# Loading v for four strips at once, in 128 partitions, in a fused attention and two-layer MLP kernel

## Chip, cores, metric

The kernel runs on one core of one Trainium2 chip. The metric is the time of one execution on the device, in microseconds (us), as the median of several executions of the same program. Less is better.

## What is computed

Sliding-window attention over 4 batches, 8 heads, 576 positions and 64 dimensions; then two MLP layers on the 2304 x 512 result. Half of the heads see the last 32 positions, the other half every fourth of the last 128 (the host reorders these heads' positions, so that they too see 32 neighbours of their own residue class).

```python
scores = np.matmul(q, k.transpose(0, 1, 3, 2)) / np.sqrt(64)
mask_plain = (rel >= 0) & (rel < 32)
mask_dil = (rel >= 0) & (rel < 128) & (rel % 4 == 0)
attn = softmax(np.where(mask, scores, -1e9))
x = np.matmul(attn, v)                      # to (2304, 512)
h = x @ w_in;  x = (h * sigmoid(1.702 * h)) @ w_out      # 512 -> 2048 -> 512
h = x @ w_in2; x = (np.maximum(h, 0) ** 2) @ w_out2      # 512 -> 2048 -> 512
```

## The kernel before

**Attention.** A batch is done in four groups (`SUBS0` for the first batch, `SUBS` for the others). A group is four strips of 32 queries that move along together: two head pairs k and the two halves u of the sequence, over `nw` = 4 or 5 windows of 32 positions. `pp` = 0 or 1 says which two head pairs (plain or dilated). Strip number a takes the partitions 32a to 32a+31 of every tile of the group; before, a = 2u + k. Groups 0 to 3 are those of the first batch, groups 4 to 7 those of the second. `attend` emits for each group:

- scores (L573): per window 8 small fp32 matmuls, of which each shows as two in the trace;
- a masked running minimum on DVE (L591), an exponential on ACT (L598), per window and head of the pair;
- reciprocals on DVE (L636, L639), a scaling on POOL for the first batch (L646, two per group), a 32x32 transpose on DVE (L660);
- values (L683): `nw`+1 steps of 8 small matmuls; step i reads the 32 keys of window i of all four strips, `v_of(a, i)`;
- evacuation of the result into the MLP's input x, in pieces: the high part by ACT or DVE (L313, L315), the low part by DVE (L700).

**v.** The keys of the first batch lie in two tiles (`v_first`, one for each pp, called `first` in the trace, as the q and k of that batch are). `load_v0` brings one strip with one load: 32 partitions, 4 packets of 1536 bytes each, eight loads for the batch (L862). Groups of later batches use one buffer `v`, filled by four loads of 32 partitions and 3 packets of 1024 bytes (`load_v`, L538); their q and k come with four loads (L530). All these loads are issued by SP, in one queue with the loads of the first layer's weights.

**MLP, layer 1.** A weight block of 128 x 512 comes as two 32-bit words per number, one load of 512 KB into one of three `raw` buffers (L379). ACT or DVE makes the top half (`c`, L313), DVE joins it (L390), ACT or DVE rounds the high part into `wp` (L313), DVE takes the low part (L324), and only then is the `raw` buffer free. There are 32 such blocks, (f, part) with f = 0 to 15; part 0 feeds L737 to L739 (hidden), part 1 feeds L794 to L796 (projection). The first layer goes through five blocks of tokens, the first with 512 tokens; the weights come in during the first. Layer 2 prepares its weights during layer 1 and runs from some 288 us on.

**Order.** Nothing is ordered by hand: a list scheduler (`Schedule`) runs over all tasks when the program is built, with costs and due times per task (`OFF`, `LEAD`, `V_FROM`, ...), and emits each engine's instructions in the order in which its plan starts them. Each engine and each queue then runs strictly in that order on the chip, with semaphore waits. Where the plan leaves PE idle before the first MLP matmul, it emits matmuls on zeros (L909, "warm" matmuls): idle time divided by `IDLE[1]`.

Of the kernel before, what the change touches and what calls it, by code (L numbers as in the profile page):

```python
# [40 lines left out]
T_ATT = 1.76  # L41
A0 = 0.23
A1 = 1.02
# [16 lines left out]
RAW_FROM = 2.32  # L60
NEXT_FROM = 20.56
OFF = (0.0, -2.48, 0.0, 0.0, 0.0, 0.0, 0.0, 0.0, 0.0, 0.0, 14.46, 0.0, -3.56, -7.14, -5.19, 0.23, -13.95, 0.0, 6.66, -22.66, 0.0, -0.52, -0.81, -0.26)
SHIFTED = ()
WARM = 256
QK_FROM = -40
QK_STEP = 4.03
V_FROM = -22.0
V_STEP = 10.52
LEAD = (22.67, 7.05, 3.53)
SPACE = 4.99  # L70
C_BUFS = 2
RAW_BUFS = 3
IDLE = (0.25, 0.22)
SPARE_POOL = (0.51, 0, 3.41)
SPARE_ACT = (0.24, 0.36, 0)
SPARE_TO = (51.64, 211.81)

# [28 lines left out]
PATIENCE = {"pe": 0.02, "act": 0.02, "dve": 0.02, "pool": 0.02, "dma": 0.02, "host": 0.02}  # L106
X_EARLY = 17.0
X_FROM = 3.56
# [147 lines left out]
def attention_mlp_mlp(  # L256
# [37 lines left out]
    q_other = [staged(f, 2 * (UQ + UK)).rearrange("p (k c) -> p k c", k=2) for f in (7, 5)]  # L294
    v_first = [staged(f, 4 * NBLK * P).rearrange("k (t d) -> k t d", t=4 * NBLK) for f in (6, 5)]
    sm_first = [staged(6, 10 * KW) for _ in range(4)]
# [210 lines left out]
    def attend(b, pp, spec, nw, want, n0, loads=None):  # L507
# [10 lines left out]
        if first:  # L518
            d_qk, d_v = loads["qk"], loads["v"]
            qk_bs = v_bs = []  # L520
        else:
            qk_bs, v_bs = [buffer("qk")], [buffer("v")]

            def load_qk(h):
                if "qk" not in m:
                    m["qk"] = qkv.tile([P, 4, 2, 6 * WIN], F32, tag="qk", bufs=1, name="qk")
                (u, w0), n = spec[h], WIN * (nw + 1)
                src = qkv_in[b, p0:p0 + 2, u, :, WIN * w0:WIN * w0 + 2 * UQ].rearrange("k p (t c) -> p k t c", t=2)
                for t in range(2):
                    nc.sync.dma_start(m["qk"][:, 2 * h:2 * h + 2, t, 0:n], src[:, :, t, 0:n])  # L530

            def load_v(h, k):
                if "v" not in m:
                    m["v"] = qkv.tile([P, 6, P], F32, tag="v", bufs=1, name="v")
                (u, w0), a, at = spec[h], WIN * (2 * h + k), UQ + UK
                c, i = (0, 0) if w0 == 0 else (1, 1)
                src = qkv_in[b, p0 + k, u, WIN * c:WIN * (c + 3), at + P * i:at + P * (i + 2)].rearrange("(c k) d -> k c d", k=WIN)
                nc.sync.dma_start(m["v"][a:a + WIN].rearrange("k (c i) d -> k c (i d)", c=3), src)  # L538

            d_qk = [  # L540
                task("dma", moved_in(512, 128 * (nw + 1)), want - 6, lambda h=h: load_qk(h), (), qk_bs, since=NEXT_FROM, count=2)
                for h in range(2)
            ]
            d_v = [
                task("dma", moved_in(96, 1024), want - 2, lambda h=h, k=k: load_v(h, k), (), v_bs, since=NEXT_FROM)
                for h in range(2) for k in range(2)
            ]

        def rows_of(a, i, wide):
            u, w0 = spec[a // 2]  # L550
            if not first:
                return m["qk"][:, a, wide, WIN * i:WIN * (i + 1 + wide)]
            w = WIN * (w0 + i)
            if pp == 0:
                return q_plain[a // 2][:, a % 2, wide, w:w + WIN * (1 + wide)]
            at = w + UQ * wide
            return q_other[u][:, a % 2, at:at + WIN * (1 + wide)]

        def v_of(a, i):
            if first:  # L560
                t = spec[0][1] + i
                v, at = v_first[pp], 4 * NBLK - 1 if t == 3 * NBLK else t % 3 * NBLK + t // 3
            else:
                v, at = m["v"], i % 3 * 2 + i // 3
# [107 lines left out]
        def values():  # L672
# [4 lines left out]
            for i in range(nw + 1):  # L677
                lo, hi = max(0, i - 1), min(nw, i + 1)
                for a in range(4):
                    rows = slice(a * WIN, (a + 1) * WIN)  # L680
                    for j in range(2):
                        js = slice(D * j, D * (j + 1))
                        T.matmul(  # L683
                            m["o"][a // 2][js, a % 2, lo * WIN:hi * WIN], v_of(a, i)[:, js],
                            pt[rows, j, max(0, i * KW - WIN):min(nw * KW, i * KW + WIN)],
# [149 lines left out]
    def spread_masks(part):  # L835
# [3 lines left out]
        if part == 0:  # L839
            G.tensor_copy(mask_band[:, 2], mask_band[:, 1])  # L840
            G.tensor_copy(mask_band[P // 2:P, 1], mask_band[P // 2:P, 0])

# [15 lines left out]

    def load_v0(pp, u, k, on):
        a, at = WIN * (2 * u + k), UQ + UK  # L860
        src = qkv_in[0, 2 * pp + k, u, :, at:].rearrange("(c q) d -> q c d", q=WIN)
        on.dma_start(v_first[pp][a:a + WIN].rearrange("q (c i) d -> q c (i d)", c=4), src)  # L862

# [3 lines left out]
    def by_act(want, fn, count=1):  # L867
# [12 lines left out]
        for u in range(2)  # L880
    ]
    v0 = [
        [
            early(moved_in(128, 1536), V_FROM + V_STEP * pp + OFF[(8, 10)[u] + pp], lambda u=u, k=k, pp=pp: load_v0(pp, u, k, nc.sync))
            for u in range(2) for k in range(2)
        ] for pp in range(2)
    ]
    loads0 = [
        {"qk": halves[0], "v": v0[0]}, {"qk": halves[0] + halves[1], "v": v0[0]},
        {"qk": others[0] + others[1], "v": v0[1]}, {"qk": others[0] + others[1], "v": v0[1]},  # L890
    ]
# [644 lines left out]
```

## Time and profile before

| | us |
|---|---|
| median of 3 runs | 813.61 (813.29 to 814.11) |
| the profiled execution | 811.69 |
| its span, first to last instruction | 809.9 |
| PE busy in the span | 796.2 |
| DVE, ACT busy | 532.2, 407.2 |
| first MLP matmul (L737) starts | 31.44 |

The span is what the views below are measured in; 1.8 us of the profiled execution lie around it. PE is busy nearly throughout. The warm matmuls count as busy too, so the share of the first 31 us says nothing of useful work. Where a view names a wait, it names what ended it.

### The profile page before, as it was taken

The page shows a single profiled execution, that of the slowest core. Times are in us where ns is not written, and L with a number is a line of the kernel's source. Part 1 is how long each engine was busy: PE and PEld are TensorE (multiplying, and loading weights), DVE is VectorE, ACT ScalarE, POOL GpSimd, SP SyncE. Part 2 cuts the span into 40 slices and gives each one's busy share as a digit, 9 for nine tenths or more (in the row PEclk, how much of TensorE's full clock was granted, in tenths as well). Part 3 has the DMA queues.
Part 4 walks back from the last instruction along what each step waited for, and adds up shares of the span by engine and source line. Part 5 has one row for each costly group of instructions (what it writes and reads, how often), then busy time and mean ns, then how long its engine had stood idle before and what let it go on. Part 6 is the DMA issues. An engine that isn't in the chain of part 4 may idle for free.

```text
span 809.9 us, 16451 instructions
## 1 busy us (share of the span) xinstructions
PE 796.2 (98%) x6559; PEld 721.8 (89%) x6559; DVE 532.2 (66%) x1162; ACT 407.2 (50%) x931; POOL 9.3 (1%) x22
## 2 busy tenths in 40 slices
PE   6899999999999999999999999999999999999998
PEld 4688887888899988888888999999999999999998
DVE  3788875443355588788887655689455698365774
ACT  6678775444444554544444255445355445354432
POOL 3000000000000000000000000000000000000000
PEclk9799999999999999999999999999999999999999
DMA  9666764221232379888576933695867687677751
GB/s 257 184 225 211 234 188 146 60 54 40 53 112 75 102 229 304 308 290 334 189 275 240 347 118 121 253 367 208 333 245 291 255 318 244 239 271 280 276 191 59
DMA packets 67964, 172.64 MB, mean 213 GB/s; under 512 B 5680, under 2 KB 43568, under 8 KB 62512
## 3 DMA queue, kind: packets, MB, share of 16 engines
q1 hardware_dynamic: 67168, 171.25, 61.4%
q8 instruction: 51, 0.84, 0.4%
q10 hardware_dynamic: 720, 0.34, 0.1%
q14 instruction: 25, 0.20, 0.1%
HBM read 132.78 MB, written 38.80 MB: 212 GB/s over the span
## 4 chain that ended last, share of the span: by engine, by line
PE 87%; DMA 8%; DVE 2%; ACT 2%; issue 1%; ACTq 0%; SPq 0%
PE ps L1225 7%; PE ps L1378 7%; PE ps L1380 7%; PE ps L1223 7%; PE ps L1224 7%; PE ps L1379 7%; PE ps L737 7%; PE ps L738 7%; PE ps L739 7%; PE ps L794 7%; PE ps L795 7%; PE ps L796 7%; DMA raw<-in_w 5%; DMA first<-in_qkv 2%; PE ps L683 2%; PE ps L573 1%
## 5 line engine op out<-in xcount | busy, mean ns | idle before, releaser
L737 PE MATMUL ps<-x,wp 128*128 128x512 f32 (+1 forms) x320 | 119.4, 373 | 0.4 <-DVE x L700 0.4
L794 PE MATMUL ps<-gh,wp 128*128 128x512 f32 (+1 forms) x320 | 119.1, 372 | 0.0
L738 PE MATMUL ps<-x,wp 128*128 128x512 f32 (+1 forms) x320 | 117.9, 368 | 0.0
L795 PE MATMUL ps<-gh,wp 128*128 128x512 f32 (+1 forms) x320 | 117.8, 368 | 0.0
L739 PE MATMUL ps<-x,wp 128*128 128x512 f32 (+1 forms) x320 | 117.8, 368 | 0.0
L796 PE MATMUL ps<-gl,wp 128*128 128x512 f32 (+1 forms) x320 | 117.7, 368 | 0.0
L1380 PE MATMUL ps<-gl,ws 128*128 128x384 f32 x336 | 112.2, 334 | 0.0
L1378 PE MATMUL ps<-gh,ws 128*128 128x384 f32 x336 | 112.2, 334 | 0.0
L1379 PE MATMUL ps<-gh,ws 128*128 128x384 f32 x336 | 112.2, 334 | 0.0
L313 ACT CAST gh<-gq 128x768 fp32r<-128x768 f32 x84 | 68.8, 837 | 70.4 <-PE ps L1379 49.5
L324 DVE TENSOR_TENSOR gl<-gq,gh 128x768 fp32r<-128x768 f32 x84 | 80.4, 957 | 28.3 <-PE ps L1380 22.1
L1223 PE MATMUL ps<-xo,ws 128*128 128x384 f32 x252 | 84.2, 334 | 0.0
L1224 PE MATMUL ps<-xo,ws 128*128 128x384 f32 x252 | 84.2, 334 | 0.0
L1225 PE MATMUL ps<-xo,ws 128*128 128x384 f32 x252 | 84.2, 334 | 0.0
L769 DVE SCALAR_TENSOR_TENSOR g<-g,ps 128x512 f32<-128x512 f32 (+1 forms) x80 | 50.4, 629 | 48.4 <-ACT g L766 47.9
L766 ACT ACTIVATE g<-ps 128x512 f32<-128x512 f32 (+1 forms) x80 | 44.0, 551 | 73.3 <-PE ps L739 72.6
L737 PEld LDWEIGHTS ps<-x,wp 128*128 128x128 f32 x320 | 60.3, 188 | 11.9 <-DVE x L700 0.9
L794 PEld LDWEIGHTS ps<-gh,wp 128*128 128x128 f32 x320 | 60.2, 188 | 10.3
L739 PEld LDWEIGHTS ps<-x,wp 128*128 128x128 f32 x320 | 60.3, 188 | 10.0
L796 PEld LDWEIGHTS ps<-gl,wp 128*128 128x128 f32 x320 | 60.3, 188 | 10.1
L795 PEld LDWEIGHTS ps<-gh,wp 128*128 128x128 f32 x320 | 60.3, 188 | 9.8
L738 PEld LDWEIGHTS ps<-x,wp 128*128 128x128 f32 x320 | 60.3, 189 | 9.7
(83 smaller groups left out, 1338.6 us busy)
## 6 DMA issues: line engine op xcount, KB each, us to landing
ws<-wo_s SPq DMA_DIRECT2D x42, 1024.0 KB, 7.0
raw<-in_w SPq DMA_DIRECT2D x64, 511.8 KB, 4.5
ws<-wi_s SPq DMA_DIRECT2D x36, 896.0 KB, 6.5
wo_s<-wt SPq DMA_DIRECT2D x16, 896.0 KB, 6.3
wi_s<-wt SPq DMA_DIRECT2D x16, 896.0 KB, 5.5
v<-in_qkv SPq DMA_DIRECT2D x48, 96.0 KB, 2.9
qk<-in_qkv SPq DMA_DIRECT2D x24, 192.0 KB, 3.8
xs<-x2d SPq DMA_DIRECT2D x12, 384.0 KB, 4.8
```

Of the source, the lines that this page charges most:

```text
L737: T.matmul(out, w_hi[:, ks], x[:, 0, k, a:z], start=(k == 0), stop=False)
L738: T.matmul(out, w_hi[:, ks], x[:, 1, k, a:z], start=False, stop=False)
L739: T.matmul(out, w_lo[:, ks], x[:, 0, k, a:z], start=False, stop=(k == KD - 1))
L794: T.matmul(out, w_hi[:, ds_], m["gh"], start=(f == 0 and a == 0), stop=False)
L795: T.matmul(out, w_lo[:, ds_], m["gh"], start=False, stop=False)
L796: T.matmul(out, w_hi[:, ds_], m["gl"], start=False, stop=(f == KF - 1))
L1223: T.matmul(out, wt[:, 0, a, ks], hi, start=(first and k == 0), stop=False, skip_group_check=True)
L1224: T.matmul(out, wt[:, 0, a, ks], lo, start=False, stop=False, skip_group_check=True)
L1225: T.matmul(out, wt[:, 1, a, ks], hi, start=False, stop=(k == 1), skip_group_check=True)
L1378: T.matmul(out, w[:, 0, j, ds_], hi, start=(first and j == 0), stop=False, skip_group_check=True)
L1379: T.matmul(out, w[:, 1, j, ds_], hi, start=False, stop=False, skip_group_check=True)
L1380: T.matmul(out, w[:, 0, j, ds_], lo, start=False, stop=(j == NPR - 1), skip_group_check=True)
```

## The change

Strip a now belongs to head pair k = a // 2 and half u = a % 2. With that, the four strips of a group lie in the input at equal distances, (k, u) by (k, u), and one load can bring the same 32 keys of all four strips: 128 partitions with one packet each. The first batch has, for each pp, three loads of 128 packets of 1536 bytes (`c` = 0 to 2) and one of 128 packets of 512 bytes (`c` = 3, the tenth window, which only groups 1 and 3 read); before, the tile held two windows twice. Later groups have three loads of 128 packets of 1024 bytes instead of four of 96. The source of such a load has the pattern 4 blocks (126,976 elements apart) x 32 rows (992 apart) x 384 elements, its destination 128 partitions x 384; before, both sides had 32 x 4 x 384.

```diff
-A0 = 0.23
+A0 = 0.22
...
-LEAD = (22.67, 7.05, 3.53)
+LEAD = (20.53, 4.91, 2.03)
...
-IDLE = (0.25, 0.22)
+IDLE = (0.25, 0.18)
...
-    v_first = [staged(f, 4 * NBLK * P).rearrange("k (t d) -> k t d", t=4 * NBLK) for f in (6, 5)]
+    v_first = [staged(f, (NWIN + 1) * P).rearrange("k (t d) -> k t d", t=NWIN + 1) for f in (6, 5)]
...
-            def load_v(h, k):
+            def load_v(c):
...
-                (u, w0), a, at = spec[h], WIN * (2 * h + k), UQ + UK
-                c, i = (0, 0) if w0 == 0 else (1, 1)
-                src = qkv_in[b, p0 + k, u, WIN * c:WIN * (c + 3), at + P * i:at + P * (i + 2)].rearrange("(c k) d -> k c d", k=WIN)
-                nc.sync.dma_start(m["v"][a:a + WIN].rearrange("k (c i) d -> k c (i d)", c=3), src)
+                at, i = UQ + UK, int(spec[0][1] > 0)
+                row = WIN * (c + i)
+                src = qkv_in[b, p0:p0 + 2, :, row:row + WIN, at + P * i:at + P * (i + 2)].rearrange("k u q d -> (k u) q d")
+                nc.sync.dma_start(m["v"][:, 2 * c:2 * c + 2].rearrange("k i d -> k (i d)"), src)
...
-                            m["o"][a // 2][js, a % 2, lo * WIN:hi * WIN], v_of(a, i)[:, js],
+                            m["o"][a % 2][js, a // 2, lo * WIN:hi * WIN], v_of(a, i)[:, js],
...
-            G.tensor_copy(mask_band[P // 2:P, 1], mask_band[P // 2:P, 0])
+            for a in (1, 3):
+                G.tensor_copy(mask_band[WIN * a:WIN * (a + 1), 1], mask_band[WIN * a:WIN * (a + 1), 0])
...
-    def load_v0(pp, u, k, on):
-        a, at = WIN * (2 * u + k), UQ + UK
-        src = qkv_in[0, 2 * pp + k, u, :, at:].rearrange("(c q) d -> q c d", q=WIN)
-        on.dma_start(v_first[pp][a:a + WIN].rearrange("q (c i) d -> q c (i d)", c=4), src)
+    def load_v0(pp, c):
+        at, i = UQ + UK, c // 3 * (NBLK - 1)
+        src = qkv_in[0, 2 * pp:2 * pp + 2, :, WIN * c:WIN * (c + 1), at + P * i:at + P * NBLK].rearrange("k u q d -> (k u) q d")
+        nc.sync.dma_start(v_first[pp][:, NBLK * c:NBLK * (c + 1) - i].rearrange("k i d -> k (i d)"), src)
...
-        {"qk": halves[0], "v": v0[0]}, {"qk": halves[0] + halves[1], "v": v0[0]},
-        {"qk": others[0] + others[1], "v": v0[1]}, {"qk": others[0] + others[1], "v": v0[1]},
+        {"qk": halves[0], "v": v0[0][0:3]}, {"qk": halves[0] + halves[1], "v": v0[0]},
+        {"qk": others[0] + others[1], "v": v0[1][0:3]}, {"qk": others[0] + others[1], "v": v0[1]},
```

`rows_of` and `v_of` follow the new numbering. Seven planner constants and eight of the 24 entries of `OFF` have new values, and the scheduler's plan comes out anew: all engines' orders change. The number of instructions does not, but for 12 v loads fewer on SP in the later groups, one POOL copy more, and 82 warm matmuls where 63 stood.

**SP's queue at the start of the program**, before (`first` at L862 are the v loads of the first batch, `raw` the weight blocks, `qk` and `v` those of group 4):

```order
L877 DMA first<-in_qkv 128x2x608 x2
L862 DMA first<-in_qkv 32x4x384 x8
L379 DMA raw<-in_w 128x2047 x3
L530 DMA qk<-in_qkv 128x2x160 x4
L538 DMA v<-in_qkv 32x3x256 x2
L379 DMA raw<-in_w 128x2047
```

and now:

```order
L878 DMA first<-in_qkv 128x2x608 x2
L863 DMA first<-in_qkv 128x1x384 x6
L379 DMA raw<-in_w 128x2047
L863 DMA first<-in_qkv 128x1x128 x2
L379 DMA raw<-in_w 128x2047 x2
L530 DMA qk<-in_qkv 128x2x160 x2
L379 DMA raw<-in_w 128x2047
L530 DMA qk<-in_qkv 128x2x160 x2
L538 DMA v<-in_qkv 128x1x256 x3
L379 DMA raw<-in_w 128x2047 x3
```

The first weight block now stands ahead of the two `c` = 3 loads, that of pp = 1 first; the v loads of group 4 stand together ahead of the fifth weight block. The blocks come as f1, f0, f3, f2 (part 0), then f0 part 1; before f0 was first. Of the later v loads, three stand ahead of the 11th block, three ahead of the 17th, and three single ones between the 29th and the 32nd.

**ACT from the exponentials of the first batch on**, before (`x` the pieces of the MLP input, `c` the top half of a weight block, `wp` its high part):

```order
L598 ACTIVATE first,st<-first,st 128x64 x33
L313 CAST x_450<-ps 128x2x3x32
L313 CAST x_454<-ps 128x2x24
L313 CAST x_450<-ps 128x2x3x32
L313 CAST x_450<-ps 128x2x32
L598 ACTIVATE first,st<-first,st 128x64 x2
L313 CAST c<-raw 128x512
L598 ACTIVATE first,st<-first,st 128x64
```

and now:

```order
L598 ACTIVATE first,st<-first,st 128x64 x27
L313 CAST x_439<-ps 128x2x3x32
L313 CAST x_439<-ps 128x2x8
L313 CAST x_444<-ps 128x2x24
L313 CAST x_439<-ps 128x2x3x32
L313 CAST c<-raw 128x512
L313 CAST x_439<-ps 128x2x32
L598 ACTIVATE first,st<-first,st 128x64 x3
L313 CAST wp<-raw 128x512
L313 CAST x_444<-ps 128x2x40
L313 CAST x_439<-ps 128x2x3x40
L313 CAST x_439<-ps 128x2x40
```

Behind these stand the last six exponentials, two top halves, a high part, and then the pieces of group 2. The evacuation of group 0 begins six exponentials earlier, and the top half of the first weight block now stands ahead of the last piece of group 0 and of the last nine exponentials. On PE the order of the useful work is the same up to the third MLP block; the warm matmuls are 13, 10, 15, 6, 8, 21 and 9 (the nine stand between the values of group 2 and the first L737), where 10, 8, 12, 14, 6, 13 and none stood. From there on group 5's scores and group 4's values come earlier among the MLP matmuls than before.

## Rows read from the trace of the kernel before

**Rows 1.** The waits of PE: us in total, times, longest.

```profile
PE ps L683 <- DMA first<-in_qkv: 3.6, 2, 3.0
PE ps L683 <- issue: 2.8, 1, 2.8
...
PE ps L737 <- DVE x L700: 0.4, 1, 0.4
```

**Rows 2.** Three stretches: length, busy us per engine, clock, DMA share, GB/s.

```profile
31.40:130.00 98.60, 98.55 (x1114) 79.65 (x1104) 79.67 (x211) 74.00 (x199) 0.00 (x0) 1.00 0.66 208
130.00:290.00 160.00, 159.60 (x2081) 138.78 (x2082) 75.31 (x299) 73.10 (x271) 0.00 (x0) 1.00 0.26 73
290.00:809.90 519.90, 516.35 (x2753) 487.38 (x2751) 362.05 (x555) 241.80 (x377) 0.00 (x0) 1.00 0.71 255
```

**Rows 3.** The chain of waits from 5 to 31 us: start, us, what.

```profile
5.24 5.82 DMA first<-in_qkv
...
11.08 8.64 DMA first<-in_qkv
...
19.76 0.90 PE ps L683 x55
...
23.37 2.77 issue
...
27.07 2.89 PE ps L909 x13
29.96 1.55 PE ps L683 x84
```

**Rows 4.** Three stretches of the opening, columns as in Rows 2.

```profile
13.50:17.00 3.50, 2.38 (x73) 1.82 (x56) 3.45 (x39) 3.35 (x21) 1.40 (x2) 1.00 1.13 228
...
20.00:22.00 2.00, 2.00 (x76) 1.30 (x60) 0.62 (x3) 0.82 (x5) 0.00 (x0) 0.66 1.03 384
...
26.10:30.90 4.80, 4.76 (x119) 3.60 (x123) 2.83 (x7) 2.10 (x6) 0.42 (x1) 0.50 0.62 180
```

**Rows 5.** SP's issues in the order of time: start, us, what, how many.

```profile
5.75 5.64 SPq L862 DMA_DIRECT2D first<-in_qkv  x8
```

**Rows 6.** ACT in the order of time: exponentials, top half, high part, pieces of x.

```profile
18.30 0.33 ACT L598 ACTIVATE first<-first,st 128x64 f32<-128x64 f32 x1
...
22.59 0.77 ACT L313 CAST c<-raw 128x512 f16<-128x512 bf16 x1
...
24.17 0.65 ACT L313 CAST wp<-raw 128x512 fp32r<-128x512 f32 x1
27.11 0.88 ACT L313 CAST x<-ps 128x240 fp32r<-128x240 f32 x4 [2.29 <-PE ps L683]
```

**Rows 7.** DVE in the order of time: transpose, join, low parts of x and weights.

```profile
6.60 0.23 DVE L591 CUSTOM_DVE_ANT_0 first<-ps,mask_band 128x64 f32<-128x64 f32 x1 [5.60 <-POOL mask_band L838]
...
22.52 0.83 DVE L660 STREAM_TRANSPOSE first<-first 128x640 f32<-128x640 f32 x1
23.39 0.69 DVE L390 SCALAR_TENSOR_TENSOR raw<-raw,c 128x512 uint32<-128x512 uint32 x1
...
28.56 0.69 DVE L324 TENSOR_TENSOR wp<-raw,wp 128x512 fp32r<-128x512 f32 x1
```

**Rows 8.** POOL in the order of time: last mask copy, scaling of a group.

```profile
4.37 0.23 POOL L841 COPY mask_band<-mask_band 64x64 bf16<-64x64 bf16 x1
...
17.67 1.40 POOL L646 TENSOR_TENSOR first<-first,st 128x320 f32<-128x320 f32 x2 [2.16 <-DVE st L639]
```

**Rows 9.** PE in the order of time: the first MLP matmul.

```profile
31.44 0.50 PE L737 MATMUL ps<-x,wp 128*128 128x512 f32 x1
```

**Rows 10.** The chain of waits from 53 to 75 us: two weight loads.

```profile
53.20 5.50 DMA raw<-in_w
...
61.73 3.40 DMA raw<-in_w
```

**Rows 11.** DMA issues between 125 and 290 us: KB each, us to landing.

```profile
v<-in_qkv SPq DMA_DIRECT2D x32, 96.0 KB, 2.5
```

More of the change, by code (lines that the diff above doesn't have):

```diff
@@ L60 @@
 RAW_FROM = 2.32
-NEXT_FROM = 20.56
-OFF = (0.0, -2.48, 0.0, 0.0, 0.0, 0.0, 0.0, 0.0, 0.0, 0.0, 14.46, 0.0, -3.56, -7.14, -5.19, 0.23, -13.95, 0.0, 6.66, -22.66, 0.0, -0.52, -0.81, -0.26)
+NEXT_FROM = 21.17
+OFF = (-0.13, -4.49, 0.0, 0.0, 0.0, 0.0, 0.0, 1.38, 0.0, 0.0, 14.46, 0.42, -1.64, -19.93, -5.19, 0.23, -13.95, 0.0, 6.66, -22.66, 0.0, 4.9, -0.81, 7.13)
 SHIFTED = ()
@@ L65 @@
 QK_FROM = -40
-QK_STEP = 4.03
+QK_STEP = 3.98
 V_FROM = -22.0
 V_STEP = 10.52
-LEAD = (22.67, 7.05, 3.53)
+LEAD = (20.53, 4.91, 2.03)
 SPACE = 4.99
@@ L72 @@
 RAW_BUFS = 3
-IDLE = (0.25, 0.22)
+IDLE = (0.25, 0.18)
 SPARE_POOL = (0.51, 0, 3.41)
 SPARE_ACT = (0.24, 0.36, 0)
-SPARE_TO = (51.64, 211.81)
+SPARE_TO = (67.29, 211.81)
 BLOCKS1 = [
@@ L106 @@
 PATIENCE = {"pe": 0.02, "act": 0.02, "dve": 0.02, "pool": 0.02, "dma": 0.02, "host": 0.02}
-X_EARLY = 17.0
+X_EARLY = 21.41
 X_FROM = 3.56
@@ L544, in attend @@
             d_v = [
-                task("dma", moved_in(96, 1024), want - 2, lambda h=h, k=k: load_v(h, k), (), v_bs, since=NEXT_FROM)
-                for h in range(2) for k in range(2)
+                task("dma", moved_in(128, 1024), want - 2, lambda c=c: load_v(c), (), v_bs, since=NEXT_FROM) for c in range(3)
             ]
         def rows_of(a, i, wide):
-            u, w0 = spec[a // 2]
+            k, h = divmod(a, 2)
+            u, w0 = spec[h]
             if not first:
-                return m["qk"][:, a, wide, WIN * i:WIN * (i + 1 + wide)]
+                return m["qk"][:, 2 * h + k, wide, WIN * i:WIN * (i + 1 + wide)]
             w = WIN * (w0 + i)
             if pp == 0:
-                return q_plain[a // 2][:, a % 2, wide, w:w + WIN * (1 + wide)]
+                return q_plain[u][:, k, wide, w:w + WIN * (1 + wide)]
             at = w + UQ * wide
-            return q_other[u][:, a % 2, at:at + WIN * (1 + wide)]
+            return q_other[u][:, k, at:at + WIN * (1 + wide)]
         def v_of(a, i):
@@ L561, in v_of @@
                 t = spec[0][1] + i
-                v, at = v_first[pp], 4 * NBLK - 1 if t == 3 * NBLK else t % 3 * NBLK + t // 3
+                v, at = v_first[pp], 3 * NBLK if t == 3 * NBLK else t % 3 * NBLK + t // 3
             else:
@@ L883, in attention_mlp_mlp @@
         [
-            early(moved_in(128, 1536), V_FROM + V_STEP * pp + OFF[(8, 10)[u] + pp], lambda u=u, k=k, pp=pp: load_v0(pp, u, k, nc.sync))
-            for u in range(2) for k in range(2)
+            early(
+                moved_in(128, 512 if c == 3 else 1536), V_FROM + V_STEP * pp + OFF[8 + pp] + (OFF[10 + pp] if c == 3 else 0),
+                lambda c=c, pp=pp: load_v0(pp, c),
+            )
+            for c in range(4)
         ] for pp in range(2)
```

## The prediction

> **What bounds the kernel now.** I read the waits of PE first. From the first MLP matmul on they hold one entry, 0.4 us on a low part of x [rows 1]; the large ones, 3.6 us for `first` loads and 2.8 us named "issue", belong to the values of the first batch (L683). The table of stretches says the same: from 31.4 us to the end PE is busy 98.55 of 98.60, 159.60 of 160.00 and 516.35 of 519.90 us, at full clock [rows 2]. So the time is the moment of the first MLP matmul, 31.44 [rows 9], plus PE's work of 778.5 us, which the change leaves as it is. It can gain only ahead of 31.44, and it can lose there or by letting PE wait later.
>
> Next, the chain of waits of the opening. The second 608 KB load ahead of v lands at 11.06 (5.24 + 5.82); the last v load is issued at 11.08 and lands 8.64 later, at 19.72, and the values of group 0 end only then, at 20.67. Those of group 1 stand still for 2.77 us and end at 27.07; 13 warm matmuls take 2.89 us, the values of group 2 take 1.55, and L737 begins [rows 3]. PE had little to do between 16 and 19.7; its granted clock is 0.50 from 26.1 to 30.9 (1.2 of 2.4 GHz), and full again from 31.4 on [rows 2, 4]. The stretches of the DMA queues show why v is late: while the v loads move (13.5 to 17.0), the 16 engines are busy all the time (share 1.13) but bring only 228 GB/s; with weight blocks and q, k (20 to 22) they bring 384 [rows 4].
>
> **The change, part by part.** *Bytes.* v of a pp shrinks from 4 x 192 KB to 3 x 192 + 64 KB.
>
> *Who carries a load.* This decides the case, and the trace does not show it. Every load of before has 32 or 128 rows as the outermost dimension of both sides, and those kept 16 engines busy [rows 4]. The new source has four blocks of 32 rows as its outermost dimension, and they lie too far apart to be one run of 128. If a load is cut along that dimension, four engines carry all of it. An engine brings 384 / 16 = 24 GB/s in the better stretch of [rows 4]; a 196.6 KB load then takes 49.2 KB / 24 = 2.05 us on four engines, against 0.51 us on sixteen. The upper bound for four is 49.2 KB at 228 / 16 = 14.25 GB/s, 3.45 us. I take 2.05, since the new loads write 128 partitions like those that reach 384 GB/s. That the cut follows the outermost dimension I give 0.85: nothing in the program asks for another, and the loads of before fit it.
>
> The Trainium skill (page "DMA: Bandwidth & Descriptors", section "Why a DMA increments its semaphore by 16 and not by 1") says that a load from SP runs on the largest number of engines up to 16 that divides the outermost dimension of both sides: 16 for 32 rows, with which this trace agrees, and 4 for the new loads, which no row here shows. By that rule the four-engine sums below hold; without it the sixteen-engine sum (first rival) does.
>
> *The queue, with four engines.* Those four work SP's queue off in order, and everything behind v needs a share of them. Counted from 11.06, the six large v loads land at 13.1, 15.2, 17.2, 19.3, 21.3 and 23.4. The first weight block (524 KB / 384 = 1.37 us) follows at 24.7, the two 64 KB v loads (0.68 each) at 25.4 and 26.1, the next blocks at 27.5 and 28.8. The issue order is no limit: six of the eight v loads of before were out within a few us of 5.75 [rows 5].
>
> *PE.* The values of group 0 need the first three: they end at some 17.9 instead of 20.67. That gain is lost at once, since the last 8 of group 1's 48 matmuls need the second 64 KB load: they end at 26.3, where 27.07 stood. Whatever the "issue" wait of 2.77 becomes lies under that wait. Behind it stand 21 warm matmuls where 13 took 2.89 - 0.11, about 0.213 each at half clock: 4.5 us, to 30.8. Group 2's values need 1.0 to 1.55 (full or half clock), then come nine warm ones, 1.0 to 1.9: L737 could begin between 32.8 and 34.2.
>
> *ACT and DVE.* Both run in order, and the top half of the first weight block, on ACT, now stands ahead of the last nine exponentials; its landing at 24.7 releases them. ACT: top half 0.77 to 25.5, last piece of x 0.3, three exponentials of 0.33 to 26.8; high part 0.65 [rows 6], group 1's pieces some 0.75, six exponentials to 30.2, two top halves to 31.8, and the high part of f0 at 32.4. Its low part takes 0.69 more, 33.1 [rows 7]. The first L737 needs the high one, the third matmul the low one. Group 2's transpose follows the 28th exponential (26.1), reciprocals, 1.40 us of POOL [rows 8], group 1's low parts and one weight low part on DVE (0.69 and 0.83 [rows 7]): 30.1, in time. So ACT and PE agree on **33.3**: 1.9 us later than now.
>
> *After 33.3.* Group 4's three v loads stand ahead of the fifth weight block: 3 x 128 KB on four engines are 3 x 1.37 = 4.1 us, where four of 96 KB at 228 GB/s took 1.7. The block lands about 2.4 us later than it could and ACT waits for it some 1 us. Its projection is due only after 36 hidden and 40 score matmuls, so I put 0.5 on the path; nothing as the lower bound, 2.4 as the upper.
>
> *The small edits.* The extra POOL copy costs 0.23 [rows 8] and the masks are then ready near 4.9, ahead of the first use at 6.60, which needs the scores [rows 7]: nothing. Five more warm matmuls ahead of the scores delay the exponentials by under 0.5 us; the wait for v to 17.2 covers that. With sixteen engines this cover is gone and it is in the first rival's time. The later v loads (12 fewer, from 128.7 us on) land 2.5 us after issue [rows 11] and with four engines about 1.1 us later; the scores, exponentials and MLP matmuls between them and their use cover that, with the DMA engines 0.26 busy [rows 2]. The swap of banks and masks leaves counts and shapes alone.
>
> *Sum,* against the profiled execution: 811.69 + 1.9 + 0.5 = 814.1. The median of the runs stands 1.92 above that execution, so the forecast is **816.0**.
>
> **Rivals.**
> 1. *Sixteen engines, faster.* If loads are dealt by the destination's 128 partitions, v lands at 0.51 us a load, the sixth at 14.2 and the first weight block at 15.5. ACT then sets the pace: 27 exponentials to 17.1 (the 33rd starts at 18.30 now [rows 6], less 6 x 0.33, plus 0.33 and the 0.45 of the warm matmuls), pieces and top half to 19.2, three exponentials and a high part to 20.8, group 1 (with its 2.77 of "issue", now bare) to 22.9, six exponentials, two top halves, a high and a low part: L737 near 27.3, 4.1 us earlier: **809.5**. For it: the bad rate of 32 partitions in [rows 4] is really removed. Against it: the pattern of the source. It decides if the first v load lands within 1.5 us of the load before it. Chance 0.15.
> 2. *Four engines, and the weights starve PE.* Blocks land 3.4 to 5.5 us after issue while PE does not wait, and the chain through the weight blocks is unbroken there [rows 10]; some 2 us of margin are thus shown, not more. Three groups of v loads stand ahead of blocks, each 2.4 us slower. If the margin is used up, up to 3 x 2.4 come on top of 1.9; I take 4.5: **820**. Against it: group 4's and 5's exponentials are moved ahead, out of the later weight stretch. Chance 0.17.
> 3. *Four engines, nothing gained or lost.* Four engines alone may run at 30 GB/s when twelve idle (1.64 us a load): block and last v load land 2.5 us earlier, ACT's chain ends near 31, L737 begins about where it does now: **813.6**, give or take 1.5. Against it: no stretch shows over 24 GB/s an engine. Chance 0.18.
>
> **How the numbers follow.** The forecast keeps 0.5, with 813.8 to 818.5 as its own range (0.5 us less to nothing after the opening, a clock that rises sooner; the 0.9 us of half clock and 2.4 us of late weights on top). Cases on both sides matter, so the range reaches into rival 1 below and past rival 2 above: **810.5 to 821**. It leaves out most of rival 1 and the 3.45 us bound (some 10 us more, under 0.03). A measurement of this kernel tells some 0.2%, 1.6 us, from no change. Faster than 812.0: rival 1 and a little of rival 3, 0.17. Within: the rest of rival 3 and the low end of the forecast, 0.28. Slower than 815.2: 0.55.
>
> **What would show it.** The v loads of the first batch land 2 us apart, not 0.5; the later ones land over 3 us after issue; GB/s of 12 to 18 us falls below 228 with few engines busy; group 0's values end near 18, group 1's near 26.5 after a wait for `first`; ACT waits for `raw` at its first top half until 24.7; L737 starts at 33.3. L737 near 27, with v loads 0.5 us apart, would prove me wrong; L737 where I say and a time over 818 would mean new waits of PE for `wp` between 40 and 80 us.

## The result, and the profile after

The changed kernel takes 824.82 us, the median of four runs (823.98 to 829.02), beside 813.45 us for the kernel before on the same chip: a ratio of 1.015, 95% interval 1.0114 to 1.0185. It is slower, as forecast, but by 11.4 us and not by 2.4: outside the range. The profiled execution took 824.99 us; its span is 823.0 where 809.9 stood. The spans differ by some 2 us more than the medians, since the profiled execution before lay 1.8 us under its median. These 13.1 us have two places: the first MLP matmul starts 3.4 us later (34.86 for 31.44), and what follows it takes 788.1 us for 778.5, 9.6 us more.

The waits of PE, to be read beside [rows 1]: us in total, times, longest.

```profile
PE ps L683 <- DMA first<-in_qkv: 6.4, 2, 6.1
PE ps L737 <- DVE g L769: 2.2, 1, 2.2
...
PE ps L794 <- ACT gh L313: 1.1, 1, 1.1
...
PE ps L794 <- DVE gh L315: 0.9, 1, 0.9
PE ps L795 <- DVE wp L324: 0.7, 1, 0.7
PE ps L794 <- ACT wp L313: 0.6, 1, 0.6
PE ps L737 <- DVE x L700: 0.5, 1, 0.5
```

The first line is the opening. All the others shown lie behind the first MLP matmul, where the kernel before had one line of 0.4 us. Two of them name `wp`, the weights. The table of stretches, columns as in [rows 2], says the same:

```profile
34.86:130.00 95.14, 92.10 (x983) 73.35 (x981) 73.36 (x191) 65.07 (x167) 0.00 (x0) 1.00 0.68 203
130.00:290.00 160.00, 156.56 (x2036) 133.86 (x2035) 72.52 (x290) 70.71 (x266) 0.00 (x0) 0.99 0.24 76
...
13.50:17.00 3.50, 2.24 (x98) 1.58 (x98) 3.37 (x38) 3.31 (x20) 1.40 (x2) 1.00 0.44 130
17.00:20.00 3.00, 2.52 (x113) 2.01 (x103) 0.94 (x6) 0.72 (x4) 0.00 (x0) 1.00 0.64 175
```

PE is idle for 3.04 us before 130 and for 3.44 between 130 and 290, where 0.05 and 0.40 stood; where the second stretch's mean clock is 0.99, another 1.6 us of work are lost. That is 7.6 us more than before. Most of the other 2 us lie in the same waits: a row of idle time starts at the modelled end of the matmul before it, 0.39 us after that one's start, while without a wait the next starts after 0.23. Counted from start to start, the ten waits cost 8.3 us and not 6.5 (0.6 for 0.4 before), which leaves 0.3 of the 9.6.

**Who carries a v load.** The DMA queues between 12 and 16.4 us, in 40 slices of 0.11 us: busy share of 16 engines in tenths, and GB/s.

```profile
DMA  2222322222222222822223222222222222222299
GB/s 112 84 98 98 112 112 84 98 98 112 112 84 98 98 112 112 233 98 98 112 84 112 84 112 112 84 112 84 112 112 84 112 84 112 112 84 112 84 223 223
```

While v alone moves, a quarter of the engines is busy and brings some 100 GB/s, 25 an engine; before, all were busy and brought 228 [rows 4]. The semaphore events of the trace count the engines. The first v load, issued at 6.00, steps its semaphore five times: once at 7.08, then four times between 12.66 and 12.83. A weight block steps its own 16 times. By the Trainium skill (page "DMA: Bandwidth & Descriptors", section "Why a DMA increments its semaphore by 16 and not by 1") the issuer writes 16 - k at once and each of the k engines adds one when its data has landed; with k = 4 that makes five steps, and the trace agrees.

**The opening.** The last step of each semaphore gives the landings: the six large loads at 12.83, 14.82, 16.75, 20.39, 22.37 and 24.41, the first weight block at 25.76, the two 64 KB loads at 26.58 and 27.53. SP's issues (the rows of the first six v loads answer to [rows 5]), three pieces of the chain of waits from 5 to 36 us that answer to [rows 3], the top half on ACT [rows 6], and the first MLP matmul [rows 9]; each block is of one view, in that order:

```profile
6.00 7.45 SPq L863 DMA_DIRECT2D first<-in_qkv  x6
13.49 2.12 SPq L379 DMA_DIRECT2D raw<-in_w  x1
15.65 1.68 SPq L863 DMA_DIRECT2D first<-in_qkv  x2
17.38 6.51 SPq L379 DMA_DIRECT2D raw<-in_w  x2
```

```profile
13.49 2.12 SPq L379
...
16.27 11.26 DMA first<-in_qkv
...
34.57 6.64 DMA raw<-in_w
```

```profile
25.84 0.76 ACT L313 CAST c<-raw 128x512 f16<-128x512 bf16 x1 [7.53 <-DMA raw<-in_w]
```

```profile
33.95 1.16 PE L913 MATMUL ps<-zeros 128*128 128x256 bf16 x9
34.86 0.48 PE L737 MATMUL ps<-x,wp 128*128 128x512 f32 x1
```

The last 64 KB load lands 11.26 us after its issue; group 1's values wait for it until 27.58. SP itself is held: two weight blocks take 6.51 us to issue. Before, the first three blocks were issued in about 0.35 us each, though not at once: each followed the landing of a v load. The block at 34.57 stands behind group 4's three v loads; without them, later in the program, a block takes some 4.2 us.

**After the opening.** The chain of waits from 55 to 140 us, weight loads and one store: start, us, what. They answer to [rows 10].

```profile
56.66 8.02 DMA raw<-in_w
...
75.53 7.54 DMA raw<-in_w
...
88.49 4.14 DMA raw<-in_w
...
117.69 8.14 DMA raw<-in_w
...
139.46 6.03 DMA x2d<-ost
```

Three weight blocks take 7.5 to 8.1 us. SP has issued three v loads right ahead of each, in the last case with blocks between them. The fourth, at 88.49, has none ahead and takes 4.14. The store at 139.46 stands behind three v loads too. The semaphores tell which part is late: of the block at 75.53 twelve steps have come by 80.50, and the last four come between 82.56 and 83.07; of the store twelve have come by 141.64, and the last four come from 145.27 on. Of the block at 88.49 all sixteen come between 91.34 and 92.62. So it is four engines' parts that are late, as many as carry v. ACT needs the buffer that it holds, in the order of time:

```profile
145.59 0.60 ACT L319 ACTIVATE ost<-ps 128x512 f32<-128x512 f32 x1 [5.74 <-DMA x2d<-ost]
146.08 0.59 ACT L766 ACTIVATE g<-ps 128x512 f32<-128x512 f32 x1
```

Behind that copy stands the g for which PE waits 2.2 us. In this trace more is lost behind the wait: from 1.5 us after it PE's clock is at its lower level (1.2 of 2.4 GHz) for a while, matmuls that started 0.23 us apart start 0.43 apart, and the 8 us from 147 on have a mean clock of 0.79, 1.7 us of work (columns as in [rows 2]). A wait as long does not always have this behind it, as a run below shows.

```profile
147.00:155.00 8.00, 7.56 (x56) 5.87 (x57) 3.06 (x5) 2.72 (x5) 0.00 (x0) 0.79 0.09 33
```

### The profile page after: what moved, and what is told of

Read it like the earlier page. It is cut to its first block, busy times and chain, and to the rows that moved or that the text cites. A ratio compares the mean times of both kernels' runs of the same rounds, so it can differ in the third digit from the quotient of the medians.

```text
span 823.0 us, 16461 instructions
## 1 busy us (share of the span) xinstructions
PE 801.7 (97%) x6578; PEld 723.7 (88%) x6578; DVE 532.9 (65%) x1163; ACT 407.1 (49%) x930; POOL 9.2 (1%) x23
## 4 chain that ended last, share of the span: by engine, by line
PE 82%; DMA 9%; DVE 4%; ACT 3%; SPq 1%; issue 1%; ACTq 0%; DVEq 0%
PE ps L1384 7%; PE ps L1228 7%; PE ps L1229 7%; PE ps L1383 7%; PE ps L1227 7%; PE ps L1382 7%; PE ps L794 7%; PE ps L795 6%; PE ps L737 6%; PE ps L796 6%; DMA raw<-in_w 6%; PE ps L739 6%; PE ps L738 6%; DMA first<-in_qkv 2%; PE ps L683 1%; ACT sm L598 1%
## 5 line engine op out<-in xcount | busy, mean ns | idle before, releaser
L737 PE MATMUL ps<-x,wp 128*128 128x512 f32 (+1 forms) x320 | 119.9, 375 | 2.7 <-DVE g L769 2.2
L738 PE MATMUL ps<-x,wp 128*128 128x512 f32 (+1 forms) x320 | 118.4, 370 | 0.0
L737 PEld LDWEIGHTS ps<-x,wp 128*128 128x128 f32 x320 | 60.4, 189 | 14.1 <-DVE g L769 2.6
L738 PEld LDWEIGHTS ps<-x,wp 128*128 128x128 f32 x320 | 60.7, 190 | 9.7
```

The lines of the kernel that those rows point to most:

```text
L737: T.matmul(out, w_hi[:, ks], x[:, 0, k, a:z], start=(k == 0), stop=False)
L738: T.matmul(out, w_hi[:, ks], x[:, 1, k, a:z], start=False, stop=False)
```

## The experiments

Times are medians, with their ratio to the kernel before on the same chip; "idle" is PE's idle time behind the first MLP matmul, up to 300 us, summed from the rows of PE in the trace (6.5 us in the changed kernel, 0.4 before).

### Rows at one distance

```diff
-        src = qkv_in[0, 2 * pp:2 * pp + 2, :, WIN * c:WIN * (c + 1), at + P * i:at + P * NBLK].rearrange("k u q d -> (k u) q d")
+        src = v_in[0, pp, c, :, P * i:P * NBLK]
...
-                src = qkv_in[b, p0:p0 + 2, :, row:row + WIN, at + P * i:at + P * (i + 2)].rearrange("k u q d -> (k u) q d")
+                src = v_in[b, pp, c + i, :, P * i:P * (i + 2)]
```

`v_in` is a second input in which the host has laid the 128 rows of each load behind one another, 992 elements apart as before.

> All v loads read from an input whose 128 rows of a load follow each other at one distance; nothing else is edited, the order of every engine stays. Theory A (everything lost comes from v loads that four engines carry): the first six v loads land about 0.5 us apart instead of 2 to 3.6, SP no longer takes 1.8 to 5 us for an issue, the first weight block lands near 16, the first L737 starts at 27 to 29 (34.86 in the changed kernel), PE's gaps behind it fall from 9.65 us to under 2, and the run takes 806 to 811. Theory B (the plan made anew is what starves PE: v loads ahead of weight blocks, f1 ahead of f0): the opening is as in A, but 5 us or more of PE gaps stay behind the first L737 and the run takes 813 to 818.

808.17 us, ratio 0.9941 (0.9924 to 0.9958). Theory A holds, and this version, the mended kernel in what follows, beats both kernels. The six large loads land 0.5 us apart (13.77 to 16.31), each stepping its semaphore 16 times; the first MLP matmul starts at 28.54; idle is 0.6 us. In the table of stretches:

```profile
28.54:130.00 101.46, 100.85 (x1116) 81.20 (x1114) 82.18 (x217) 74.00 (x198) 0.00 (x0) 1.00 0.67 214
130.00:290.00 160.00, 160.00 (x2085) 138.93 (x2084) 75.78 (x299) 72.64 (x270) 0.00 (x0) 1.00 0.24 74
```

The order of every engine is that of the changed kernel. So it was not the plan alone that starved PE: it was this plan with loads that take four times as long (1.97 us for 0.5). On PE the gain is smaller than the medians say: the span is 807.3 for 809.9, and the first MLP matmul starts 2.9 us earlier.

### Four and eight blocks

```diff
-    vrows = np.zeros((B, 2, 4, P, 992), np.float32)
+    vrows = np.zeros((B, 2, 4, 8, 32, 992), np.float32)
...
-        src = v_in[0, pp, c, :, P * i:P * NBLK]
+        src = v_in[0, pp, c, :, 0:16, P * i:P * NBLK]
```

Against the version with rows at one distance: 8 blocks of 16 rows, each followed by a gap of 16 rows. For four blocks the array is (B, 2, 4, 4, 64, 992) and the rows are 0:32. The later groups' `src` is cut in the same way.

> All v loads read 8 blocks of 16 rows with a gap between the blocks, where the changed kernel reads 4 blocks of 32; the packets and their targets stay. Theory A (a load is cut along the outermost dimension of its source): eight engines carry a load, the first six land about 1.0 us apart, the first L737 starts between that of the run with rows at one distance and 34.86, near 30, and the run takes 808 to 814. Rival (the number of blocks does not decide; gaps between blocks or anything else in the addresses does): landings 2 us apart as with four blocks and 820 to 825, or 0.5 us apart and the time of the run with rows at one distance.

812.67 us, ratio 0.999 (0.9971 to 1.0009). The first MLP matmul starts at 29.61, idle is 1.2 us. Each v load steps its semaphore nine times, one and eight; the six land at 11.96, 13.15, 14.81, 16.16, 17.84 and 19.34, 1.5 us apart and not 1.0, with the first weight block moving on the other engines meanwhile. Theory A, with eight engines that were slower than forecast.

> All v loads read from the new input, as in the runs with rows at one distance and with eight blocks, but laid out as 4 blocks of 32 rows with a gap between them. Theory A (the outermost dimension of the source decides how many engines carry a load): as the changed kernel, v loads 2 us apart, first L737 at 34 to 35.5, 822 to 827. Rival (the new input, its place or its neighbours in memory, is what made those runs fast): first L737 at 28 to 30, 806 to 813.

825.28 us, ratio 1.0159 (1.0137 to 1.018); first MLP matmul at 35.41: theory A. The new input is not what made the others fast. One row each of the stretch 11 to 16.4 us, sixteen engines, eight, and four:

```profile
11.00:16.40 5.40, 4.10 (x177) 3.18 (x175) 3.72 (x43) 4.75 (x30) 2.47 (x4) 1.00 0.96 326
```

```profile
11.00:16.40 5.40, 4.19 (x176) 3.14 (x174) 4.30 (x50) 5.36 (x33) 2.58 (x4) 1.00 0.98 247
```

```profile
11.00:16.40 5.40, 4.14 (x177) 3.17 (x175) 4.30 (x51) 5.36 (x34) 2.58 (x4) 1.00 0.28 103
```

The last two numbers of a row are the DMA share and the GB/s. With eight, the share is full because a weight block has the other eight.

### The first batch alone, and the later groups alone

```diff
-        src = qkv_in[0, 2 * pp:2 * pp + 2, :, WIN * c:WIN * (c + 1), at + P * i:at + P * NBLK].rearrange("k u q d -> (k u) q d")
+        src = v_in[0, pp, c, :, P * i:P * NBLK]
```

That is the first run, with `load_v` as in the changed kernel; the second has the other hunk of the version with rows at one distance, in `load_v`, alone.

> Only the eight v loads of the first batch read rows at one distance; those of later groups keep the four blocks. Theory A in two places (each group of four-engine loads costs where it stands): first L737 at 27 to 29 as with all loads, but the later groups' loads still hold weight blocks back, so 4 to 9 us of PE gaps stay behind it: 812 to 818. Theory C (the later waits only follow from the late start of the weight stream): the gaps behind the first L737 fall to under 2 us and the run takes 806 to 811, as with all loads.

> Only the v loads of the later groups read rows at one distance; the first batch keeps the four blocks. Theory A in two places: the first L737 stays at 34.5 to 35, the PE gaps behind it fall from 9.65 us to under 3: 814 to 818. Theory C (the later waits follow from the late start): the gaps stay at 6 us or more and the run takes 820 to 825.

First batch alone: 822.38 us, ratio 1.0115 (1.0079 to 1.0152). Later groups alone: 813.84 us, ratio 1.001 (0.9996 to 1.0024), a little below what theory A gave it. In the stretches:

```profile
28.73:130.00 101.27, 97.08 (x998) 76.95 (x996) 75.05 (x203) 68.34 (x185) 0.00 (x0) 0.98 0.67 205
130.00:290.00 160.00, 156.27 (x2041) 133.86 (x2040) 71.82 (x290) 70.47 (x265) 0.00 (x0) 0.99 0.22 68
```

```profile
35.52:130.00 94.48, 94.48 (x1002) 76.78 (x999) 78.07 (x207) 70.51 (x189) 0.00 (x0) 1.00 0.70 218
130.00:290.00 160.00, 160.00 (x2083) 138.50 (x2081) 74.42 (x297) 73.18 (x271) 0.00 (x0) 1.00 0.25 74
```

With only the opening mended, L737 starts at 28.7, but 7.9 us of idle stand behind it and the time is above the forecast range; with only the later loads mended it starts at 35.5 and PE is never idle again. Theory C falls: the later waits do not follow from the late start. They are even dearer after an earlier start: behind the first L737 the span has 791.1 us here, 788.1 in the changed kernel, 778.7 with all loads mended. Of these 3.0 us 1.4 are idle time, and the rest goes with a second stretch at the lower clock (mean 0.91 between 80 and 100 us, for 1.00). I read the idle time as weight blocks that come at their own pace, so that an MLP which begins earlier waits longer for them; no run separates it further.

### Four blocks only from group 8 on

```diff
+                src = v_in[b, pp, c + i, :, P * i:P * (i + 2)] if b == 1 else src
```

This stands behind the old `src` of the later groups; the first batch has rows at one distance.

> Rows at one distance for the v loads of the first two batches (groups 0 to 7), four blocks from group 8 on (137 us and later). Theory A: first L737 near 28.6, no waits for weights; the one wait that stays is that for g near 140 us, behind the v loads of group 8, 2 to 3.2 us with what follows it: 809.5 to 812. Rival (four-engine loads cost as much wherever they stand): 814 or more. Second rival (they cost nothing once the weights of the first layer are in): 807 to 809.

811.8 us, ratio 0.9988 (0.9972 to 1.0004): theory A, 3.6 us more than with all loads mended. L737 (here L738) starts at 28.03. No wait for weights is left, one for x has 1.0 us (two with 0.6 in all where all loads are mended), and the wait for g is there, 3.2 us (one row of PE's waits, and ACT in the order of time):

```profile
PE ps L738 <- DVE g L770: 3.2, 1, 3.2
```

```profile
134.28 0.60 ACT L319 ACTIVATE ost<-ps 128x512 f32<-128x512 f32 x1 [6.42 <-DMA x2d<-ost]
```

The clock does not fall behind this longer wait; the 8 us from 136 on show its full level:

```profile
136.00:144.00 8.00, 7.86 (x94) 6.29 (x95) 4.42 (x21) 3.75 (x10) 0.00 (x0) 1.00 0.09 24
```

The two runs with waits of 2.3 us for g (the store on ACT's queue, the 64 KB loads early) show 1.00 behind them as well. The run with the first batch alone, with a wait of 2.5 us, shows 0.79. So the 1.7 us of clock in the changed kernel's trace are not the price of every such wait, and no run here isolates what decides it.

### The store on ACT's queue

```diff
-                    nc.sync.dma_start(x2d[d][:, at:at + blk["n"]], blk["ost", d][:, 0:blk["n"]])
+                    nc.scalar.dma_start(x2d[d][:, at:at + blk["n"]], blk["ost", d][:, 0:blk["n"]])
```

> The changed kernel with its four-engine v loads; only the stores of the first layer's result (x2d<-ost) are issued by ACT's queue instead of SP's. Theory A (the 2.2 us wait of PE for g at 145 us is a store that stands behind three v loads in SP's queue and keeps the ost buffer, ACT waits for that buffer, and g comes late): that wait falls under 0.5 us, the other waits between 40 and 135 us stay, and the run takes 820.5 to 822.5. Rival (g is late for another reason, or the next wait takes over): the wait stays over 1.5 us and the run takes 823.5 to 826.

824.99 us, ratio 1.0154 (1.0123 to 1.0185): the rival. ACT still waits for the store:

```profile
147.00 0.60 ACT L319 ACTIVATE ost<-ps 128x512 f32<-128x512 f32 x1 [5.58 <-DMA x2d<-ost]
```

The store issued at 140.37 lands 6.55 us later, beside 6.03 in SP's queue. Twelve of its semaphore steps have come by 142.57, the last four come between 146.06 and 146.91. So the v loads are the cause, as the run before shows, but not the order in SP's queue: the store's parts on four busy engines take their time there, whoever issued it. The Trainium skill (page "DMA: Bandwidth & Descriptors", section "Issuing engines are not separate DMA queues") says that DMAs end up on the same 16 DMA engines, whichever engine started them, and interleave there. The trace agrees: the third v load, beside the store, now lands 7.4 us after its issue in place of 6.1.

### The later loads on POOL's queue

```diff
-                nc.sync.dma_start(m["v"][:, 2 * c:2 * c + 2].rearrange("k i d -> k (i d)"), src)
+                nc.gpsimd.dma_start(m["v"][:, 2 * c:2 * c + 2].rearrange("k i d -> k (i d)"), src)
```

> The changed kernel with its four-engine loads; those of the later groups are issued by POOL's queue instead of SP's, so no weight block and no store stands behind them in a queue, and they may start earlier. Theory Q (what costs is the order in one queue): the opening stays at 34.5 to 35.5, PE gaps behind the first L737 fall from 9.65 to under 4 us, 815 to 819. Rival S (a weight block needs a share of the same four engines, whatever queue the v loads come from): gaps of 6.5 us or more stay, 822 to 826.

824.78 us, ratio 1.0146 (1.0116 to 1.0176), idle 7.7 us: by the time and the idle time the rival, but not by its mechanism. PE's waits hold no weights and no g any more; two others, above all, took their place:

```profile
PE ps L683 <- DVE first L660: 3.8, 1, 3.8
PE ps L683 <- DMA v<-in_qkv: 2.8, 3, 2.2
```

POOL issues a v load and then waits 4 to 6.5 us before the next; two of them stand between its scalings of group 3, whose transpose comes late. The v loads of the later groups come late themselves. And POOL's loads go through a queue of another kind (the DMA queues, 138 to 146 us: packets, MB, share):

```profile
q0 software_dynamic: 206, 0.15, 9.6%
```

So this run does not tell queue from engines, and it is left as inconclusive.

### Strips

```diff
+        for a in range(4):
-        nc.sync.dma_start(v_first[pp][:, NBLK * c:NBLK * (c + 1) - i].rearrange("k i d -> k (i d)"), src)
+            nc.sync.dma_start(v_first[pp][WIN * a:WIN * (a + 1), NBLK * c:NBLK * (c + 1) - i].rearrange("k i d -> k (i d)"), src[a])
```

The same for the later groups.

> Every v load of the changed kernel is issued as four loads of 32 partitions and one packet each, from the old input, so that 32 rows are the outermost dimension; order and bytes stay. Theory A (only the number of engines matters): as with rows at one distance, PE gaps behind the first L737 under 2 us. But SP issues 32 loads instead of 8 ahead of the weight blocks, some 0.5 us each, so the sixth v group is out at 18 instead of 9 and the first L737 comes at 30 to 32.5: 809 to 813. Rival (the gain of the run with rows at one distance needs the single load over 128 partitions; in strips the rate falls back to 228 GB/s and the issues of later groups hold weight blocks up): first L737 after 32.5 or PE gaps over 3 us, 813 to 818.

833.03 us, ratio 1.0237 (1.0202 to 1.0271): both expectations missed in the time, on the slow side; the first L737 and the idle time are as the rival said. SP is the limit in the opening (its issues in the order of time):

```profile
6.90 18.20 SPq L865 DMA_DIRECT2D first<-in_qkv  x24
```

That is 0.76 us a load and not 0.5, though most issues take 0.42: three take 1.4 to 1.7, and from 10.33 to 13.78 SP waits for the landing of the load eight before, whose semaphore the next one uses again. The DMA engines are 0.31 to 0.37 busy between 11 and 22 us, the first MLP matmul starts at 37.5, and idle behind it is 10 us. Sixteen engines alone are no cure if SP has to issue four loads for one.

### A plan with true costs

```diff
-                task("dma", moved_in(128, 1024), want - 2, lambda c=c: load_v(c), (), v_bs, since=NEXT_FROM) for c in range(3)
+                task("dma", 3 * moved_in(128, 1024), want - 2, lambda c=c: load_v(c), (), v_bs, since=NEXT_FROM) for c in range(3)
...
-                moved_in(128, 512 if c == 3 else 1536), V_FROM + V_STEP * pp + OFF[8 + pp] + (OFF[10 + pp] if c == 3 else 0),
+                3 * moved_in(128, 512 if c == 3 else 1536), V_FROM + V_STEP * pp + OFF[8 + pp] + (OFF[10 + pp] if c == 3 else 0),
```

> The changed kernel with its four-engine loads, but the scheduler's cost of every v load is three times what it was (1.96 us for the large ones instead of 0.65, as they land 1.97 us apart), so the plan is made for loads as long as they are. Theory P (most of the 9.6 us behind the first L737 is a plan that counts on loads three times faster): the first L737 at 33 to 36, PE gaps behind it under 4 us, 815 to 820. Rival (the four engines are simply too busy between 30 and 140 us, whatever the order): gaps of 6.5 us or more stay, 821 to 827.

819.55 us, ratio 1.0075 (1.0055 to 1.0094): theory P. L737 starts later than forecast, at 37.35, but idle is 2.5 us, all of it before 50 us, and none of it for weights or g:

```profile
37.35:130.00 92.65, 90.13 (x920) 73.35 (x914) 70.24 (x191) 66.18 (x172) 0.00 (x0) 0.98 0.63 195
130.00:290.00 160.00, 160.00 (x2075) 138.48 (x2074) 76.86 (x303) 74.91 (x285) 0.00 (x0) 1.00 0.26 81
```

About half of the loss goes with a plan that takes a v load for what it is, 1.97 us and not 0.65. The other half stays in this plan, most of it in its opening: behind the first L737 the span has 780.3 us, 1.8 more than in the kernel before.

The costs of the other case, set the same way:

> Rows at one distance for all v loads, sixteen engines, and the scheduler's costs of the v loads set to what the first such run showed (0.51, 0.33 and 0.18 us instead of 0.65, 0.47 and 0.28). Theory P: the plan was already near enough to such loads, 806 to 810, no difference to the run without the new costs. Rival: the constants belong to one plan and any other is worse: 811 or more.

818.1 us, ratio 1.0059 (1.0037 to 1.0081): the rival, and 9.9 us more than with the old costs. The first MLP matmul comes at 26.93, 1.6 us earlier than with the old costs, but 3.1 us of idle follow before 300 us, and one wait in the second layer:

```profile
PE ps L1227 <- ACT ost L319: 4.9, 1, 4.9
```

I read that as other constants that belong to one plan; no run shows which. So the 5 us that true costs gave above are the difference of two plans too, and not only of their costs.

### The 64 KB loads early

```diff
+        if c == 3:
+            return
+        load_v0_part(pp, c)
+        if c == 2:
+            load_v0_part(pp, 3)
```

> The changed kernel, but the 64 KB load c = 3 of each pp is issued right behind that pp's c = 2, and so ahead of the first weight block; nothing else moves. Group 1 then has its values from 17.5 on instead of 27.5, and the first weight block lands near 25.4 instead of 25.76. Theory PE (the 1.6 us by which the first L737 came later than forecast are group 1's values and the 21 warm matmuls behind them): the first L737 comes at 33 to 34, and no fourth v load lands 3.6 us after the third, since no weight block moves beside it; 822.5 to 824. Rival (ACT's chain from the first weight block on sets it): the first L737 stays at 34.5 to 35, 824 to 826.

828.36 us, ratio 1.019 (1.0162 to 1.0217): both missed. L737 starts at 37.46, 2.6 us later than in the changed kernel. ACT shows why:

```profile
29.10 0.76 ACT L313 CAST c<-raw 128x512 f16<-128x512 bf16 x1 [10.70 <-DMA raw<-in_w]
```

The weight block, now behind all v loads, lands at 29.02 and not at 25.4, and L737 follows the top half by 8.4 us (9.0 in the changed kernel). I had it wrong that no block would move beside v: three blocks are issued from 16.89 on, twelve engines take their parts at once, and v on the other four slows. The last three large loads land at 21.66, 24.47 and 27.04, 2.6 to 2.8 us apart. The packet records of the trace say the same: a v packet of 1536 bytes takes 65 ns while v moves alone, and 74 to 108 ns in the mean of each us from 18 to 26.

## Why the prediction was right or wrong

**Right: who bounds, and who carries v.** Four engines carry a load, at 25 GB/s each (24 forecast), and the source's outermost dimension decides it: sixteen, eight and four engines were shown on one input, with one order of instructions. The first three landings were within 0.5 us of the forecast (12.83, 14.82, 16.75 for 13.1, 15.2, 17.2), and group 0's values end at 17.5 (17.9).

**The opening was mis-sized: +3.4 for +1.9.** From the fourth load on each landing is 1.0 to 1.4 us late: 20.39 for 19.3, the first weight block 25.76 for 24.7, the last 64 KB load 27.53 for 26.1. The step that failed here is that v holds its rate when another load is on the other twelve engines. In the 18th and 19th us a v packet takes 83 and 147 ns in the mean, in place of 65, while the first weight block moves, and the fourth load needs 3.6 us. The rest follows as forecast: group 1's values end at 27.98 (26.3), 21 warm matmuls take 4.6 us (4.5). PE and ACT agree to half a us, as they did in the forecast: PE is through its nine warm matmuls at 34.86, and DVE ends the last low part in time for it at 34.55. Moving the 64 KB loads forward therefore could not help. The 3.4 us are one execution's: three other runs with the same loads in the first batch start L737 at 33.99 (the store on ACT's queue), 34.33 (POOL's queue) and 35.52 (later groups mended).

**"The issue order is no limit" was wrong as a fact, cheap in effect.** SP was held up to 5 us by an issue. That kept the second weight block from the idle twelve engines between 19.4 and 22.7 us, and the third behind it; the run with the 64 KB loads early, where those blocks did move, was not faster.

**The step that cost most: "I put 0.5 on the path".** In place of this 0.5 stand 9.6 us behind the first L737, a good third of them waits that follow on weight blocks. The block behind group 4's loads was forecast 2.4 us late, with a projection due much later. For that block the size was right, 6.64 us where others take 4.2, and PE did not wait for it. But three blocks behind later v loads take 7.5 to 8.1 us, and PE's idle times at 67 to 69, 83 and 134 us follow on them in the chain of waits. That was rival 2, with a chance of 0.17 and a price of 4.5. The size was about right: these waits come to 3.3 us of idle, 4.0 from start to start. What rival 2 lacked of the measured time is the wait for g, with the clock behind it, and the 1.5 us by which the opening was later than forecast. The waits of weights in the trace before had little margin [rows 10]; I read that as a reason for a rival and not for the forecast.

**"The scores, exponentials and MLP matmuls cover that": wrong.** The prediction put the later v loads at nothing. Group 8's loads cost 2.2 us of wait, and in this trace 1.7 of clock, although their own use was covered. I asked who waits for v, and not who shares its engines. The store behind them keeps a buffer, ACT waits for the buffer, PE for ACT. No rival had this. The run with four blocks from group 8 on has this wait and one of 1.0 us for x, no fall of the clock, and takes 3.6 us more than the mended kernel.

**Rival 1,** sixteen engines, was forecast at 809.5 with L737 at 27.3; the mended kernel shows it at 808.17 with L737 at 28.54. That the time comes so near is in part luck: L737 starts 2.9 us earlier than before and not 4.1, and the spans differ by 2.6, while the medians differ by 4.9. The idea of the change, one load over 128 partitions, is worth 0.6%; the pattern of its source turned that into a loss of 1.5%.

**A sum that does not come out.** The forecast's own bounds, 813.8 and 818.5, do not follow from the terms named with them: 816.0 with the 0.9 of half clock and 2.4 in place of 0.5 is 818.8, and for a clock that rises sooner no size is given. The stated range, 810.5 to 821, is wider and does not hang on them.

What stays open: how much of the 9.6 us is the plan and how much the four engines. The plan with true costs has 1.8 us of them left with loads on four engines, but it also starts the MLP 2.5 us later, and each plan tried brings constants made for another.

## What to carry to other kernels

Count the outermost dimension of both sides of a load before its bytes: with four blocks, a load has four engines, and a load in a good order over all partitions can be the slow one. A load on few engines is paid by everything that needs those engines, weights and stores alike, and a store issued from ACT's queue paid it as one from SP's did; look for whoever holds a buffer meanwhile. And when a load gets another duration, try the planner with its true cost, but measure the new plan: that won 5 us with four engines and lost 10 with sixteen.

## What the runs showed of the hardware

- A semaphore shows how many engines carry a load: 1 + 4 steps, 1 + 8, or 16. It also shows whose part is late: where v loads stood ahead on four engines, twelve of sixteen steps come first, and 1.7 to 5 us later the last four.
- SP is held while it issues when large loads ahead of it stand on four engines: 1.8 us for a v load from the fourth on, up to 5.0 us for a weight block (changed kernel). Up to 300 us in the kernel before and in the mended one, the median of all issues is 0.42 us, the longest of a weight block 1.15 and the longest of all 1.8.
- While a weight block moves on the other twelve engines, v packets of 65 ns take up to 147 ns in the mean of a us.
- Eight engines beside a weight block brought a 196.6 KB load in 1.5 us, 16.4 GB/s an engine, where four alone had 25.
- 24 loads of 49 KB took SP 18.2 us to issue with the DMA engines a third busy; SP, not the bytes, set the pace.
- PE's clock fell behind a wait of 2.2 us in the changed kernel and stayed at its full level behind one of 3.2 us in another run: mean clock 0.79 and 1.00 over the 8 us behind.
